# Chunk-selected attention into a gMLP block on one core: scores and masks in row halves, bounds of eight heads in eight tiles, x^T by DMA transpose, and a fixed order table

## The chip, the cores, the metric

One NeuronCore of a Trainium2 chip runs the whole kernel. The metric is device time in microseconds (us). A kernel is run several times, and each run is slow when it is over 1.5% above the fastest run of the same kernel, otherwise fast. A ratio is the mean time of one kernel's fast runs over that of the other's fast runs of the same rounds, so it is not quite the ratio of the medians quoted beside it. The kernel before has a profile (262.9 us) whose run isn't among the times listed.

Engines: PE is the matmul engine (PEld its weight loads), DVE the vector engine, ACT the activation engine, POOL the general engine, and SP issues most DMAs.

## The reference, cut to what matters

```python
# attention: B=4, H=8, S=768, D=64, chunks of 32 keys, the best 6 chunks of each query
k_min, k_max = k_chunks.min(3), k_chunks.max(3)
ub = sum(maximum(q * k_min, q * k_max), -1)          # bound of every (query, chunk)
ub = where(causal_by_chunk, ub, -1e9)
top_chunks = argsort(ub)[..., -6:]
scores = q @ k.T / 8, masked to chosen chunks and to causal positions
attn = softmax(scores) @ v
# gMLP on x = heads side by side, (4, 768, 512)
h = gelu(x @ w_in); u, v = halves of h
v_s = w_sg @ (layernorm(v) * g_ln) + b_sg
out = x + (u * v_s) @ w_out
```

Two heads of one batch make a *pair*; there are 16 pairs and 4 batches. Queries 0 to 191 have at most 6 chunks and need no selection. The other 576 do.

## The kernel before

Every piece of work is an `Op` with an engine, an estimated cost, and what it reads and writes. While the program is built, a scheduler plays these operations forward with the estimated costs and fixes each engine's order. Engines then run in that order and wait on semaphores, so a late operation holds up everything behind it on its engine. The rule is greedy: each engine takes what can start first. Priority decides only among operations that could start within 0.02 us of each other.

```python
# schedule(), cut: one engine's choice
for i in ready[e]:
    t = max(rt[i], free[e])                     # inputs there, engine free
    if o.alloc is not None and o.alloc.slot is None:
        s = slot_for(o.alloc, t)                # earliest free PSUM buffer of the allowed ones
        if s is None: continue
        t = max(t, s[0] + 0.15)
    cands.append((t, o.prio, i))
tmin = min(c[0] for c in cands)
best = min((c for c in cands if c[0] <= tmin + 0.02), key=lambda c: c[1])
```

PSUM has two large score buffers (PSC) and four small ones (PSG). Stages may use only some of the small ones, for instance (0, 1) for transposes and (2, 3) for the gMLP.

The scores carry the mask inside the contraction. `QA` has 64 rows of q and 24 rows of "this chunk is not chosen" (D); `KA` has 64 rows of k and 24 indicator rows. One matmul of 88 rows does a piece of a head. The second head of the pair uses 128 rows. The exp then runs over 1024, 1024 and 640 columns.

```python
# head(), cut
kt_, qt_, rows = (KA[w], QA[w], slice(0, 64 + NC)) if i == 0 else (KB[w], QB[w], slice(0, 128))
e.matmul(t.ap()[:, o:o + n], kt_[rows, 128*kb:128*kb+128], qt_[rows, q0:q0+n], start=True, stop=True)
...
# select(g), cut: bounds of 4 heads in 4 tiles of 64 rows x 32 columns, f32
for m in range(2):
    for j in range(4):
        w, lo = (2*g + j//2) % 4, 64 * (j % 2)
        e.matmul(t.ap()[32*j:32*j+32, 0:n], W[w][lo:lo+64, m, :], rhs, tile_position=(lo, 32*j), ...)
...
# xtrans(b, dk), cut: x^T by 6 PE transposes and a DVE copy
e.matmul(t.ap(BF16)[:, 128*j:128*j+128], XS[...], identB[:], is_transpose=True)
d.tensor_copy(xT[b % 2][:, dk, :], t.ap(BF16)[:, 0:S])
...
# weights(h), called after head(h): two of 14 weight loads wait for the first exp of head h
reads=[("tick", h)]
```

The softmax here doesn't subtract the row's maximum and nothing guards it: scores larger than these inputs give would overflow.

## Time and profile before

| | before |
|---|---|
| device time, median (range) | 267.67 us (266.84 to 268.25, 3 runs) |
| span of the profile | 262.9 us |
| busy PE / DVE / ACT / POOL | 225.0 / 197.7 / 153.4 / 76.9 us |
| start of the first and of the last exp | 23.8 and 227.9 us |

The first view is the page: busy time by engine, then the span in 40 slices of 6.6 us. A digit is the busy share in tenths. PEclk is the clock that PE was granted.

```profile
span 262.9 us, 5801 instructions
...
PE 225.0 (86%) x2242; PEld 140.2 (53%) x2258; DVE 197.7 (75%) x561; ACT 153.4 (58%) x232; POOL 76.9 (29%) x99
...
PE   8886488987996599998899899997998998689874
...
PEclk9999689999999569999999999999999999999999
DMA  7999999998999904856751443122101031100033
```

PE is at 9 in 18 of the 40 slices. No engine is full throughout, yet PE and DVE both carry most of the span, and the clock falls twice. The same as a table of stretches: stretch, its length, then busy us (and instructions) of PE, PEld, DVE, ACT, POOL, then granted clock, DMA share, GB/s.

```profile
core 0: us, PE busy (x) PEld busy (x) DVE busy (x) ACT busy (x) POOL busy (x), PEclk, DMA share, GB/s
...
20.00:40.00 20.00, 13.11 (x138) 7.96 (x137) 15.27 (x52) 11.82 (x20) 9.17 (x12) 0.83 1.06 208
...
80.00:100.00 20.00, 14.85 (x125) 9.90 (x123) 13.64 (x29) 12.34 (x19) 6.96 (x7) 0.74 0.67 123
...
140.00:160.00 20.00, 18.91 (x217) 13.53 (x211) 18.20 (x54) 14.29 (x22) 7.16 (x8) 1.00 0.38 92
```

PE loses time in 20-40 and 80-100 us, at a clock of 0.83 and 0.74. PE's busy time overstates its work, because matmuls overlap: six of 384 columns stream in 0.98 us, though each is listed with some 335 ns. DMA is near full for the first 14 slices, 92 us (208 GB/s in 20-40 us).

Three stages can be told apart by the exps. From the view of one source line (count, min/median/max ns, first and last start in us, shapes):

```profile
L682 ACT ACTIVATE E<-PSC x96: 698/1023/1074, 23.8 to 227.9; 128x1024 bf16<-128x1024 f32 x64, 128x640 bf16<-128x640 f32 x32
```

So the *start* takes 23.8 us, the *middle* 204.1 us, and the *end*, after the last exp starts, 35.0 us. The chain of waits through the start (start, length, what) is mostly DVE work in a row:

```profile
10.22 0.88 DVE KA L491
...
16.47 2.19 PE PSG L613 x32
...
19.20 1.47 DVE m_0 L629 x18
...
22.28 0.77 DVE QA L640
...
23.86 0.77 DVE QA L640
```

It runs on through four transposes of 0.77 us that write the mask rows into QA and QB. Score matmuls start at 23.11 us and the exp at 23.8 us.

### The profile page before, as it was taken

The numbers are of one execution on the slowest core, as the hardware profiler recorded it, in microseconds if no ns is written. First come the engines' busy times: TensorE is split into PE (matmuls) and PEld (weight loads), VectorE is DVE, ScalarE is ACT, GpSimd is POOL, SyncE is SP. The second block draws the span as 40 slices with busy tenths as digits, with TensorE's granted clock in tenths as the row PEclk, the third lists the DMA queues.
The fourth block names the chain that finished last, engine by engine and source line by source line (L and its number), as shares of the span: only waits on it lengthen the run. The fifth ranks groups of instructions, "written<-read, shape, count | busy, mean of one in ns | idle before, by whom it ended". The sixth has DMA issues, their size and how long they took to land.

```text
span 262.9 us, 5801 instructions
## 1 busy us (share of the span) xinstructions
PE 225.0 (86%) x2242; PEld 140.2 (53%) x2258; DVE 197.7 (75%) x561; ACT 153.4 (58%) x232; POOL 76.9 (29%) x99
## 2 busy tenths in 40 slices
PE   8886488987996599998899899997998998689874
PEld 3444256665743378655555577566445765434431
DVE  6949579787558668989677988886588876467883
ACT  1444848977649545655784974658757645846000
POOL 3353728653201424222212433134210211202000
PEclk9999689999999569999999999999999999999999
DMA  7999999998999904856751443122101031100033
GB/s 167 201 225 202 205 221 197 235 227 175 199 209 160 212 19 109 228 132 182 163 122 43 100 100 135 51 95 55 38 6 24 2 122 58 64 0 0 0 123 120
DMA packets 84652, 32.39 MB, mean 123 GB/s; under 512 B 77232, under 2 KB 80912, under 8 KB 84624
## 3 DMA queue, kind: packets, MB, share of 16 engines
q1 hardware_dynamic: 82608, 29.26, 48.1%
q0 software_dynamic: 2016, 2.75, 6.4%
q8 instruction: 18, 0.29, 0.5%
q14 instruction: 10, 0.08, 0.1%
HBM read 24.77 MB, written 6.29 MB: 118 GB/s over the span
## 4 chain that ended last, share of the span: by engine, by line
PE 50%; DVE 32%; ACT 9%; issue 6%; POOL 1%; POOLq 1%
PE PSG L794 9%; PE PSG L814 8%; PE PSC L677 8%; PE PSG L613 7%; DVE W L546 5%; ACT E L682 5%; DVE vhat L767 5%; PE PSG L751 4%; PE PSG L696 4%; DVE vsT L801 3%; PE PSG L777 3%; DVE uT L805 3%; DVE m_1 L629 2%; DVE XS L713 2%; PE PSC L463 2%
## 5 line engine op out<-in xcount | busy, mean ns | idle before, releaser
L682 ACT ACTIVATE E<-PSC 128x1024 bf16<-128x1024 f32 (+1 forms) x96 | 84.5, 920 | 44.7 <-PE PSC L677 44.1
L686 POOL TENSOR_SCALAR_AFFINE_SELECT E<-E 128x768 bf16<-128x768 bf16 x32 | 28.5, 892 | 59.9 <-ACT E L682 59.6
L794 PE MATMUL PSG<-wsgT,vhat 128*128 128x384 bf16 x192 | 36.6, 335 | 4.9 <-DVE vhat L767 3.0
L546 DVE TENSOR_REDUCE W<-PSG 128x12 f32<-128x384 f32 x64 | 33.1, 543 | 7.5 <-PE PSG L540 7.3
L677 PE MATMUL PSC<-QB,KB 128*128 128x128 bf16 (+1 forms) x224 | 26.0, 253 | 2.7 <-ACT E L682 2.7
L677 PE MATMUL PSC<-QA,KA 88*128 88x128 bf16 (+1 forms) x224 | 24.8, 249 | 3.4 <-ACT E L682 2.6
L794 PEld LDWEIGHTS PSG<-wsgT,vhat 128*128 128x128 bf16 x192 | 18.3, 100 | 17.6 <-DVE vhat L767 3.0
L801 DVE SCALAR_TENSOR_TENSOR vsT<-PSG,glnT,bsgbc 128x384 f32<-128x384 f32 x32 | 19.7, 614 | 7.6 <-PE PSG L794 7.5
L814 PE MATMUL PSG<-woutb,uT 128*128 128x512 bf16 x88 | 21.8, 380 | 3.9 <-DVE uT L805 3.3
L777 PE MATMUL PSG<-xT,winb 128*128 128x384 bf16 x128 | 23.8, 327 | 0.4 <-DVE xT L727 0.3
L696 PE MATMUL PSG<-vx,E 128*128 128x65 bf16 x480 | 20.4, 195 | 4.1 <-ACT E L682 2.7
L696 PEld LDWEIGHTS PSG<-vx,E 128*128 128x128 bf16 x480 | 18.0, 99 | 10.0 <-ACT E L682 5.6
L751 PE MATMUL PSG<-winb,xT 128*128 128x512 bf16 x90 | 21.6, 379 | 1.3 <-DVE xT L727 0.9
L575 PE MATMUL PSG<-identF,qn 128*128 128x128 f32 x96 | 16.1, 283 | 6.7 <-ACT KB L551 3.6
L755 ACT ACTIVATE vgb<-PSG 128x512 f32<-128x512 f32 x24 | 14.1, 598 | 13.1 <-PE PSG L751 13.1
L820 DVE TENSOR_TENSOR osb<-PSG,XS 128x512 f32<-128x512 f32 x24 | 16.6, 691 | 6.4 <-PE PSG L814 5.9
L677 PEld LDWEIGHTS PSC<-QA,KA 88*128 88x128 bf16 x224 | 16.3, 99 | 9.5 <-ACT E L682 4.6
L580 ACT ACTIVATE qT<-PSG 128x384 f32<-128x384 f32 x32 | 15.5, 496 | 9.5 <-PE PSG L575 9.4
L782 ACT ACTIVATE uT<-PSG 128x384 bf16<-128x384 f32 x32 | 15.6, 490 | 9.1 <-PE PSG L777 8.8
L598 POOL CAST vx<-vn 128x768 bf16<-128x768 f32 x16 | 13.2, 830 | 24.1 <-PE PSG L703 19.2
L677 PEld LDWEIGHTS PSC<-QB,KB 128*128 128x128 bf16 x224 | 15.9, 100 | 7.8 <-ACT E L682 4.9
L758 DVE BATCH_NORM_STATS2 stats<-vgb 128x6 f32<-128x512 f32 x24 | 16.0, 681 | 4.7 <-ACT vgb L755 4.7
(69 smaller groups left out, 343.7 us busy)
## 6 DMA issues: line engine op xcount, KB each, us to landing
kn<-in_k_dram SPq DMA_DIRECT2D x32, 192.0 KB, 3.6
qn<-in_q_dram SPq DMA_DIRECT2D x32, 192.0 KB, 3.6
vn<-in_v_dram SPq DMA_DIRECT2D x32, 192.0 KB, 3.5
out_dram<-osb SPq DMA_DIRECT2D x24, 256.0 KB, 2.0
vgb<-in_moe_w_sg_dram POOLq DMA_DIRECT2D x6, 192.0 KB, 5.9
QB<-QA SPq DMA_DIRECT2D x12, 96.0 KB, 2.2
KB<-KA SPq DMA_DIRECT2D x12, 96.0 KB, 3.0
winb<-in_moe_w_in_dram POOLq DMA_DIRECT2D x4, 256.0 KB, 5.9
```

What stands on the lines that cost most here:

```text
L546: P.op("dve", lambda d, t=t, m=m, op=op, hf=hf: d.tensor_reduce(W[w][:, m, 12 * hf:12 * hf + 12], t.ap()[:, 0:TG].rearrange("p (c x) -> p ...
L613: r = e.matmul(t.ap()[32 * j:32 * j + 32, 0:n], W[w][lo:lo + 64, m, :], rhs, start=(m == 0), stop=(m == 1), tile_position=(lo, 32 * j))
L677: r = e.matmul(t.ap()[:, o:o + n], kt_[rows, 128 * kb:128 * kb + 128], qt_[rows, q0:q0 + n], start=True, stop=True, skip_group_check=True)
L682: P.op("act", lambda e, t=t, c0=c0, c1=c1: e.activation(E[es][:, c0:c1], t.ap()[:, 0:c1 - c0], ACTF.Exp, scale=SCALE), act(c1 - c0), reads ...
L686: P.op("pool", lambda g: g.affine_select(ev, ev, pattern=[[0, NT], [1, 128]], compare_op=ALU.is_ge, fill=0.0, base=0, channel_multiplier=- ...
L696: r = e.matmul(t.ap()[:, 65 * qb:65 * qb + 65], E[es][:, a:a + 128], vx[w][:, kb, i, :], start=first, stop=False, skip_group_check=True)
L751: r = e.matmul(t.ap()[:, 0:F], xT[s][:, dk, 128 * qt:128 * qt + 128], winb[:, dk, F:DFF], start=(dk == 0), stop=(dk == NDK - 1))
L777: r = e.matmul(t.ap()[:, 0:TG], winb[:, dk, 128 * fb:128 * fb + 128], xT[s][:, dk, TG * tg:TG * tg + TG], start=(dk == 0), stop=(dk == NDK ...
L794: r = e.matmul(t.ap()[:, 0:TG], vhat[s][:, sb, 128 * fb:128 * fb + 128], wsgT[:, sb, TG * tg:TG * tg + TG], start=(sb == 0), stop=(sb == N ...
L801: P.op("dve", lambda d, t=t, fb=fb, tg=tg, vs=vs: d.scalar_tensor_tensor(vsT[vs][:], t.ap()[:, 0:TG], glnT[:, fb:fb + 1], bsgbc[:, TG * tg ...
L814: r = e.matmul(t.ap()[:, 0:DM], gT[s][:, fb, 128 * qt:128 * qt + 128], woutb[:, fb, :], start=(fb == 0), stop=(fb == NF - 1))
L820: P.op("dve", lambda d, t=t, qt=qt, os_=os_: d.tensor_tensor(osb[os_][:], t.ap()[:, 0:DM], XS[:, (b % 2) * NT + qt, :], op=ALU.add), dve(D ...
```

## The change

The intent, as its words give it (`window` is how many loads may be in flight; `filler` is how many dummy matmuls PE runs before an operation): both heads of a pair are done at once in the two halves of PE's rows, the mask is added by separate matmuls, bounds of eight heads use eight tiles, three of four x^T go to the DMA, and the order of all 1171 operations comes from a table found offline. Cut to its core:

```diff
+PLAN = dict(order=[0, 2, 47, 13, 6, ...],        # 1171 operations; cut
+            slots=[4, 5, 6, 7, ...],             # PSUM buffer of every tile, in that order; cut
+            window=4, filler={50: 7, 42: 3, 59: 11, 35: 7, 73: 7, 113: 4})
-    def schedule(self):                          # the greedy rule
+    def place(self, order, slots, window):       # takes the table as it is
 # scores of a pair, in six chunks of 2 x 512 columns (the last 2 x 128)
-    e.matmul(t.ap()[:, o:o+n], kt_[rows, ...], qt_[rows, ...], start=True, stop=True)
+    for i in range(2):
+        rows = slice(64*i, 64*i+64)
+        e.matmul(ap(t)[:, i, o:o+n], KT[r][rows, ...], QT[r][rows, q0:q0+n],
+                 start=True, stop=not masked, tile_position=(64*i, 0))
+    for i in range(2):
+        if masked:                               # queries from 192 on
+            e.matmul(ap(t)[:, i, o+m0-q0:o+n], IND[jj][rows, ...], D[ds][tb][rows, ...],
+                     start=False, stop=True, tile_position=(64*i, 0))
 # bounds: after two groups of four heads, groups of eight
+    ts = [PsumTile(ANY) for _ in banks]
+    ... tile_position=(64*i, 32*c)
 # x^T
+    if b > 0:
+        e.dma_start_transpose(xT[:, dk, :].rearrange("p (j x) -> p j x", x=128), flat(b, dk))
 # small PSUM buffers: every stage may take any of the four
-    t = ps_g.tile((2, 3))
+    t = PsumTile(ANY)                            # ANY = (4, 5, 6, 7)
 # weight loads, now declared before the first exp
+    for i in range(14):
+        weight(i)                                # reads=[("tick", 0)]
+    small_weights()                              # reads=[("tick", 0)]
```

Further: six sets of K, Q and V instead of four, one x^T and one normalized-V buffer instead of two, no copies KB<-KA and QB<-QA and their DMAs, and fewer memsets and copies at the start.

## The prediction

> **What bounds it now.** No single engine. The busy table gives PE 225 us (86%), DVE 198, ACT 153, POOL 77 of a 263 us span, but PE's figure contains pipeline latency: in the timeline six 384-column matmuls stream in 0.98 us (163 ns each) although one is listed as 335 ns. My estimate of PE work from stream spacings: gMLP 92 us, scores 36, probabilities times V 21, q/k transposes 20, bounds 15.5, x^T 5, w_sg 2; about 191 us. The other 70 us is dependency time:
> - Start: the first exp comes at about 23.8 us (timeline), behind a serial DVE chain that ends in four 0.77 us transposes into QA/QB (chain of waits).
> - First 80 us: the windows view shows DMA share about 1.0 at some 205 GB/s. About five pairs of q/k/v (1.18 MB each) and 5.4 MB of weights must arrive before the first gMLP: estimated 55 us. No order removes that.
> - Middle: granted clock 0.83 in 20-40 us and 0.74 in 80-100 us (windows); around 86-94 us PE waits on vhat.
> - Tail: last exp ends 228.6 us, then 34 us of the last gMLP alone.
>
> **What the change does.**
> - Bounds: 16 f32 matmuls with 288 columns take 0.97 us on four tiles; eight heads in eight tiles should take the same. Groups fall from eight to two of four heads and three of eight: 15.5 to 9.7 us of PE, minus 6.
> - Scores: mask rows move out of the contraction into separate matmuls, two heads running in row halves. Per pair 2688+2432 columns instead of 2x2688: at most 5% less if halves overlap. The Trainium skill, "TensorEngine Tiling (Array Packing)", Key Properties, says tiles run in parallel but changing mode drains the array. The trace agrees on both: the four bound tiles share 0.24 us slots, and the first weight load after a bound group starts about 0.14 us after the stream's end, after 0.47 us idle of the loader. With 96 score chunks and up to two switches each I estimate plus 15 to 30 us of PE, partly hidden. This is the main cost.
> - x^T: 12 of 16 PE transposes (0.34 us of PE) and DVE copies (0.55 us) go to DMA: PE minus 4, DVE minus 6.6. It happens when DMA share is below 0.65; costs a few us latency before each gMLP.
> - DVE also loses QA/QB transposes and setup copies: about 198 to 182.
> - ACT: same exp elements and instruction count (153 to about 150). Causal select on POOL: same elements.
> - Copies KB<-KA, QB<-QA and their small DMAs disappear.
> - Order: all four small PSUM buffers open to all stages, six K/Q/V sets, measured durations behind the table. I expect the largest gain here: middle stalls of about 40 us shrink by 10 to 15.
>
> **Sum (estimate).** Start -3, bounds/x^T/DVE -6 to -8 on the chain, order -12, mode switches +4: about -19 of the profile. Predicted time **247 us**, 80% range **231 to 263**. Faster by over 2%: 0.80; within 2%: 0.13; slower by over 2%: 0.07.
>
> **What would show it.** First exp before 22 us; score matmuls of two heads starting within a few ns, chunk streams about 0.4 us; an idle gap of 0.1 to 0.3 us around each score chunk; eight bound matmuls sharing a slot; DVE busy near 182, ACT near 150; fewer PE waits on ACT and vhat; tail still about 33 us; DMA still saturated to about 60 us.
>
> **What would make it wrong.** Row halves not overlapping (PE +34 us: no gain); larger drain; DMA transposes blocking loads in the SP queue or landing late; a fixed order mistimed so that in-order engines wait on each other; conversely a well packed order reaching 230 or less.

## The result, and the profile after

| | before | after |
|---|---|---|
| device time, median (range) | 267.25 us (263.39 to 268.25, 4 runs) | 241.84 us (238.98 to 245.76, 4 runs) |
| ratio of fast runs | | 0.902 (95%: 0.891 to 0.913) |
| span of the profile | 262.9 us | 236.6 us |
| start / middle / end by the exps | 23.8 / 204.1 / 35.0 us | 30.0 / 167.9 / 38.7 us |
| busy PE / DVE / ACT / POOL | 225.0 / 197.7 / 153.4 / 76.9 us | 216.4 / 182.3 / 149.0 / 72.0 us |

The medians after are of two fast and two slow runs, so the interval is wide. The profile after is a fast run. Its page:

```profile
span 236.6 us, 6378 instructions
...
PE 216.4 (91%) x2596; PEld 132.6 (56%) x2596; DVE 182.3 (77%) x531; ACT 149.0 (63%) x224; POOL 72.0 (30%) x99
...
PE   7739699999899399999999999999999999999974
...
PEclk9967999999999999999999999999999999999999
DMA  7899999999989999999740302043301411302143
```

```profile
core 0: us, PE busy (x) PEld busy (x) DVE busy (x) ACT busy (x) POOL busy (x), PEclk, DMA share, GB/s
...
20.00:40.00 20.00, 17.28 (x221) 11.27 (x223) 14.53 (x48) 11.07 (x20) 5.44 (x9) 0.99 1.08 208
...
80.00:100.00 20.00, 18.06 (x260) 12.21 (x258) 16.59 (x35) 17.63 (x26) 7.80 (x9) 1.00 0.98 200
...
140.00:160.00 20.00, 20.00 (x348) 12.19 (x348) 17.12 (x71) 14.83 (x20) 7.41 (x10) 1.00 0.22 52
```

```profile
L572 ACT ACTIVATE E<-PSC x96: 378/1023/1138, 30.0 to 197.9; 128x1024 bf16<-128x1024 f32 x80, 128x256 bf16<-128x256 f32 x16
```

PE is now at 9 in 32 of the 40 slices, and busy for the whole of 140-160 us. PEclk is at 9 from the fifth slice (24 us) on; in 80-100 us it is 1.00 in place of 0.74. DMA is near full for 19 slices, 112 us, in place of 92. The six buffer sets in place of four would let the loads run ahead so; no run isolates that.

By stages the 26.3 us of the span come from the middle alone: minus 36.2 us there, plus 6.2 us at the start, plus 3.7 us at the end. The chain of waits shows what happened at the start:

```profile
4.72 10.59 DMA qn<-in_q_dram
...
15.40 1.51 PE PSG L434 x6
...
22.85 2.19 PE PSG L495 x32
...
25.70 1.46 DVE m L513 x18
```

The second pair's q was issued at about 4.7 us and landed at 15.3, after 10.59 us. In the kernel before, that pair's k was transposed from 10.7 us and its q from 12.5 us; after, its q from 15.4 us and its k from 19.7 us. In between, POOL issued six of the weight loads (4.8 to 10.7 us), which share the DMA engines (DMA share 0.95 in 0-20 us). The chain also still has one mask transpose of 0.78 us (28.28 us) before the first exp, as before had.

That the weights go so early has its reason in the tick. The weight loads name it as something that they read, and should so wait for the exp that writes it. But they are declared before the exp that writes it, so there is no writer to wait for. The dependence turns round: the exp that writes the tick has to wait until all 16 readers are done. The built program says so; this is its ACT order (position, line, instruction, semaphores; cut):

```
29 L231 EventSemaphore [waits d_winb3,d_woutb2]
30 L231 EventSemaphore [waits d_winb2,d_winb0]
31 L231 EventSemaphore [waits d_woutb3,d_winb1]
32 L231 EventSemaphore [waits d_gln,d_woutb1]
33 L231 EventSemaphore [waits d_bsg,d_woutb0]
34 L572 Activation E<-PSC 128x2x512 [waits s_pe]
```

It is the eighth exp in ACT's order, not the first. In the trace it starts at 39.13 us, and the five waits before it take 0.04 us each: in this table the loads had landed by then. (The six w_sg loads aren't listed: the wait for PE covers them, as PE has transposed them by then.) So what delays the start is that nothing holds the weights back, not this wait.

The row halves overlap as hoped. A timeline of PE (start, length with latency, what; "x2" merges two):

```profile
100.75 1.14 PE L688 MATMUL PSG<-wsgT,vhat 128*128 128x384 bf16 x6
101.82 0.23 PE L556 MATMUL PSC<-QT,KT 64*128 64x128 bf16 x2
101.89 0.22 PE L563 MATMUL PSC<-D1Z,IND 64*128 64x128 bf16 x1
...
102.06 0.27 PE L556 MATMUL PSC<-QT,KT 64*128 64x256 bf16 x2
102.17 0.24 PE L563 MATMUL PSC<-D1Z,IND 64*128 64x192 bf16 x1
...
102.34 0.55 PE L434 MATMUL PSG<-identF,kn 128*128 128x128 f32 x3
```

Two heads' matmuls start together, each pair of 128 columns takes 0.06 us, and the w_sg group before it streams six times 0.163 us. That group ends its stream at 100.75 + 0.98 = 101.73 us; the scores begin at 101.82. The last mask matmul, 192 columns, ends its stream at about 102.25, and the next transpose begins at 102.34. So a change of array mode costs about 0.09 us either way. From 40 us on, the trace has 103 changes between the full array and the row halves that follow a bf16 matmul; their median gap is 95 to 98 ns, against 3 ns between matmuls of the full array. The Trainium skill, "TensorEngine Tiling (Array Packing)", Key Properties, says that changing the mode drains the array; this trace agrees and gives the size.

Bounds before (four heads) and after (eight heads), from the same view:

```profile
137.01 0.69 PE L613 MATMUL PSG<-qT,W 64*32 64x288 f32 x8
137.52 0.67 PE L613 MATMUL PSG<-rT,W 64*32 64x288 f32 x8
138.12 1.47 PE L777 MATMUL PSG<-xT,winb 128*128 128x384 bf16 x8
```

```profile
107.41 0.71 PE L495 MATMUL PSG<-qT,W 64*32 64x288 f32 x16
107.92 0.69 PE L495 MATMUL PSG<-rT,W 64*32 64x288 f32 x16
108.55 0.34 PE L556 MATMUL PSC<-QT,KT 64*128 64x384 bf16 x2
```

The interval to the next work is 1.11 us for 16 instructions before and 1.14 us for 32 after. Eight tiles run at the price of four.

### The profile page after: what moved, and what is told of

It is laid out like the page before. It is cut to its first block, busy times and chain, and to the rows that moved or that the text cites. A ratio compares the mean times of both kernels' runs of the same rounds, so it can differ in the third digit from the quotient of the medians.

```text
span 236.6 us, 6378 instructions
## 1 busy us (share of the span) xinstructions
PE 216.4 (91%) x2596; PEld 132.6 (56%) x2596; DVE 182.3 (77%) x531; ACT 149.0 (63%) x224; POOL 72.0 (30%) x99
## 4 chain that ended last, share of the span: by engine, by line
PE 71%; DMA 18%; DVE 4%; ACT 3%; SPq 2%; issue 1%
PE PSG L688 13%; PE PSC L556 9%; PE PSG L708 8%; DMA qn<-in_q_dram 8%; PE PSG L590 8%; PE PSG L434 7%; PE PSG L672 7%; PE PSG L645 7%; PE PSC L563 6%; DMA vn<-in_v_dram 5%; PE PSG L495 4%; DMA D1Z<-D1Y 2%; ACT E L572 2%; DMA kn<-in_k_dram 2%; DMA xT<-XS 2%; PE PSC L362 1%
## 5 line engine op out<-in xcount | busy, mean ns | idle before, releaser
L556 PE MATMUL PSC<-QT,KT 64*128 64x128 bf16 (+2 forms) x448 | 42.5, 246 | 4.8 <-ACT E L572 2.4
L578 POOL TENSOR_SCALAR_AFFINE_SELECT E<-E 128x512 bf16<-128x512 bf16 (+1 forms) x32 | 28.1, 884 | 31.1 <-ACT E L572 30.9
L556 PEld LDWEIGHTS PSC<-QT,KT 64*128 64x128 bf16 x448 | 20.3, 94 | 22.6 <-ACT E L572 9.3
L471 POOL CAST QT<-qT 128x768 bf16<-128x768 f32 x16 | 14.4, 898 | 47.0 <-ACT qT L465 35.7
L708 PE MATMUL PSG<-woutb,uT 128*128 128x512 bf16 x96 | 23.7, 380 | 1.3 <-DVE uT L699 1.3
L590 PE MATMUL PSG<-vx,E 128*128 128x65 bf16 x672 | 24.8, 194 | 0.0
L590 PEld LDWEIGHTS PSG<-vx,E 128*128 128x128 bf16 x672 | 22.2, 98 | 3.6 <-issue 1.4
L676 ACT ACTIVATE uT<-PSG 128x384 bf16<-128x384 f32 x32 | 15.5, 491 | 12.5 <-PE PSG L672 12.1
L434 PE MATMUL PSG<-identF,qn 128*128 128x128 f32 x96 | 15.1, 289 | 7.6 <-DMA qn<-in_q_dram 5.6
L450 ACT ACTIVATE KT<-PSG 128x384 bf16<-128x384 f32 x32 | 15.2, 498 | 10.0 <-DVE W L447 9.7
L699 DVE TENSOR_TENSOR uT<-vsT,uT 128x384 bf16<-128x384 f32 x32 | 20.9, 654 | 0.6
```

Of the source, the lines that this page charges most:

```text
L434: r = e.matmul(ap(t)[:, 128 * j:128 * j + 128], src[:, 3 * hf + j].rearrange("p i d -> p (i d)"), identF[:], is_transpose=True)
L556: x = e.matmul(ap(t)[:, i, o:o + n], KT[r][rows, 128 * kb:128 * kb + 128], QT[r][rows, q0:q0 + n], start=True, stop=not masked, tile_posit ...
L578: P.op("pool", lambda g, ev=ev, nd=nd: g.affine_select(ev, ev, pattern=[[0, 2], [0, nd // 128], [1, 128]], compare_op=ALU.is_ge, fill=0.0, ...
L590: x = e.matmul(ap(t)[:, 65 * qb:65 * qb + 65], E[es][:, i, a:a + 128], vx[r][:, kb, i, :], start=first, stop=(kb == qb), skip_group_check= ...
L699: P.op("dve", lambda d, fb=fb, tg=tg, vs=vs: d.tensor_tensor(uT[s][:, fb, TG * tg:TG * tg + TG], vsT[vs][:], uT[s][:, fb, TG * tg:TG * tg ...
L708: r = e.matmul(ap(t)[:, 0:DM], uT[s][:, fb, 128 * qt:128 * qt + 128], woutb[:, fb, :], start=(fb == 0), stop=(fb == NF - 1))
```

## The experiments

Twelve kernels ran on three chips. Where a number is compared across chips, the ratio to before is used. The kernel after stands at 0.902 by its own runs. e4, which turned out to be its equal in time, stands at 0.909.

### e1: the new operations in the old order

The edit puts the operations of the kernel after through the greedy rule of the kernel before, and stores the resulting order, buffers and filler as its table.

```diff
-    order=[0, 2, 47, 13, ...], slots=[4, 5, 6, 7, ...],        # the table of the change
-    filler={50: 7, 42: 3, 59: 11, 35: 7, 73: 7, 113: 4})
+    order=[...], slots=[...],                                  # the greedy rule's
+    filler={31: 9, 40: 3, 50: 14, 59: 6, 71: 4})
```

> The kernel after with its operations unchanged, but order, buffer slots and filler taken from the greedy rule of the kernel before instead of the searched table. Theory A (most of the gain is the searched order): 254 to 264 us, so less than half of the 25 us remains. Rival B (the new operations make the gain, any sensible order will do): 247 us or less. The 96 exps should again be spread over 190 us or more from first to last under A, and 175 us or less under B (before 204, after 168).

Measured: 284.12 us median, ratio 1.070 (1.064 to 1.076). That is 42 us more than e4 on the same chip, and slower than before.

```profile
L573 ACT ACTIVATE E<-PSC x96: 377/1024/1142, 35.3 to 243.6; 128x1024 bf16<-128x1024 f32 x80, 128x256 bf16<-128x256 f32 x16
```

The middle is 208.3 us, no shorter than before's 204.1. Rival B falls. Theory A's direction holds, but not its size: the new operations in the old order do not keep a part of the gain; they lose 18 us. The whole gain, and more, came with the table. Changes of array mode are not what makes e1 slow: its PE order has 107 of them, the table's 146. One thing isn't separated: e1 keeps the turned tick, so the greedy rule had to place that exp behind all 16 weight loads. The greedy rule without the tick was not run.

### e2: scores without row halves and mask matmuls (wrong numbers on purpose)

```diff
-    e.matmul(ap(t)[:, i, o:o+n], KT[r][rows, ...], QT[r][rows, ...], tile_position=(64*i, 0), stop=not masked)
-    e.matmul(... IND ..., ... D ...)             # the mask
+    e.matmul(ap(t)[:, i, o:o+n], KT[r][:, ...], QT[r][:, ...], start=True, stop=True)   # all 128 rows
```

> Wrong numbers on purpose: each score matmul uses all 128 rows (5376 columns a pair, no mask matmuls, no row halves), same table. It takes away 2 changes of array mode for each of 96 chunks, 0.09 us each by the trace (17 us of PE together), and adds about 1.7 us of columns. Theory: PE is what limits from 80 us on, so the time falls by 8 to 16 us, to 226 to 234. Rival: the drains hide behind other waits, time within 2 us of the kernel after.

Measured: 233.89 us, ratio 0.878 (0.874 to 0.883); 7.9 us less than e4 on the same chip. The result was wrong. The table lets score chunks follow each other at places, so that PE changes mode not 192 but 146 times (147 runs of one mode in its order). e2 keeps 16 of these, for the bounds, and takes away 130. At 0.09 us that is 12 us; 7.9 us plus the 1.7 us of added columns is about 10 us. The rest may hide behind waits, or in the clock: in 80-120 us the profile of e2 was granted 0.91, that of e4 1.00. So row halves cost this kernel 8 us against a score of the same size on the full array. A correct version of that would again need masks and both heads' rows copied together, as in the kernel before; it was not built.

### e3: one half after the other in program order

```diff
-    for (o, n, kb, q0) in todo:
-        for i in range(2): ...score...
-        for i in range(2): ...mask...
+    for i in range(2):
+        for (o, n, kb, q0) in todo: ...score... ...mask...
```

> Same matmuls as the kernel after and right numbers, but in each chunk all of head 0's come before all of head 1's, so that neighbours in the queue share a row half and cannot overlap. If the overlap of the halves is what makes the scores affordable: score streams double from 34 to 68 us and the time rises by 20 to 34 us, to 262 to 276, no better than before. Rival (halves overlap little, or PE has slack): rise under 8 us.

Measured: 244.36 us, ratio 0.918 (0.913 to 0.924), 2.6 us above e4 on the same chip. This was a miss, but not because overlap is worth little. The edit did not take it away:

```profile
29.82 0.23 PE L557 MATMUL PSC<-QT,KT 64*128 64x128 bf16 x2 [1.80 <-DVE D0X L521]
29.88 0.22 PE L561 MATMUL PSC<-D0X,IND 64*128 64x128 bf16 x2
29.94 0.22 PE L557 MATMUL PSC<-QT,KT 64*128 64x128 bf16 x1
```

In this first chunk the program order, in the built program too, is score and mask of head 0, then score and mask of head 1. The trace has the scores of both heads at 29.82 us and both masks at 29.88. The second head's matmul started before the first head's mask that stands ahead of it. The Trainium skill, "TensorE: Matmul & The Clock Gate", Part 3, says that matmuls keep strict program order in start and end. This trace differs in the start, and the measurement decides: matmuls of another row half went ahead. (Ends of matmuls are modelled in these profiles and say nothing here.) e12 repeats the test properly.

### e4: without the tick

```diff
-            after = [("tick", 0)]
+            after = []
```

> The reads of the tick are dropped from the 16 weight loads. In the kernel after they were declared before the exp that writes the tick, so they do not hold the weights back: instead one exp of the first pair waits for all 16 loads. Same table. Theory: that wait is short (the searched order put the weights early because of it), time lower by 0 to 3 us; first exp still at about 30 us since the second pair's q and k still share the DMA with the weights. Rival (the wait holds up the start): lower by 4 to 7 us.

Measured: 241.80 us, ratio 0.909 (0.904 to 0.914). The wait of the exp costs nothing in this table, as its 0.04 us waits in the trace after suggested. The rival falls. First exp 31.3 us, as expected.

### e5: without the tick, and the weights later in the table

```diff
             after = []                           # as in e4
     order=...                                    # the 16 weight loads one after every second q/k/v load
                                                  # from the 9th on; w_sg transposes before the first hidden matmul
```

> Tick reads dropped as in e4, and the table changed for the weights alone: the 16 weight loads and the w_sg transposes are taken out of the first 30 us; w_sg and w_in come between the loads from the 9th q/k/v load on, one for every two, b_sg, g_ln and w_out after them, the w_sg transposes right before the first hidden matmul. Theory (the slow start is the weights sharing the DMA with the second pair's q and k): first exp at 20 to 25 us in place of 30; the total falls by 2 to 6 us, to 236 to 240, less than the start because the first gMLP still waits for the same bytes. Rival (the first 70 us are bound by total DMA bytes, the start is hidden): earlier first exp, total within 1.5 us of 241.8, or later if the moved transposes stall PE.

Measured: 239.64 us, ratio 0.8965 (0.893 to 0.900). This is the fastest correct kernel. It ran on another chip than e4, so its margin of about 1% is likely rather than shown.

```profile
L573 ACT ACTIVATE E<-PSC x96: 378/1024/1131, 20.9 to 196.9; 128x1024 bf16<-128x1024 f32 x80, 128x256 bf16<-128x256 f32 x16
```

The start fell from 30.0 to 20.9 us, which shows that the weights made it slow. But 9 us at the start gave some 2 us in all, since the middle grew from 167.9 to 176.0. Its chain of waits tells why:

```profile
12.80 6.60 DMA kn<-in_k_dram
...
22.93 10.93 DMA qn<-in_q_dram
33.88 4.20 DMA kn<-in_k_dram
```

Up to 54 us the chain goes on so: loads of q, k or v are its long links. The same bytes must come before the same work; attending to the first pair earlier only leaves PE waiting later (in 40-60 us it is busy for 14.54 us, after for 19.72). Both theories had a share: the cause of the late start was the weights, and the rival was right that the total is bound by bytes there.

### e6 and e11: x^T of all batches back on PE and DVE

```diff
-            if b > 0:
-                P.op("sp", lambda e: e.dma_start_transpose(...))
+            if False:
     order=..., slots=...     # 12 x (6 PE transposes, a DVE copy) put in; e11 where a buffer stays free longer
```

> x^T of batches 1 to 3 back on PE and DVE (6 transposes of 0.056 us and a 0.55 us copy for each of 12 tiles), put into the searched table two PE steps after the place of the DMA. Theory: PE is the limit from 80 us on, so the time rises by 3 to 6 us (PE 4.1, DVE 6.6), to 245 to 248. Rival (the DMA transposes delay the gMLP by their 3.3 us landing; the wait at 165 us in the trace is one): no rise, or a fall of up to 3 us.

> As e6 (x^T of batches 1 to 3 on PE and DVE again) but placed with more care: the transposes where a buffer stays free longest, the copy after two more DVE operations. If e6's 12 us were mostly mistimed waits of my insertion: 246 to 250 us. If the work itself, 10.7 us on two nearly full engines, costs it: 252 us or more.

Measured: e6 253.91 us, ratio 0.949 (0.944 to 0.953). e11 247.13 us over all runs, two of which are slow; its ratio of fast runs is 0.919 (0.911 to 0.926). So e6 came out above both of its expectations. e11 met its first by all runs, and its two fast runs (244.11 and 245.14 us) are just below it. The same operations at slightly different places of the table differ by about 8 us. In e6 the weight loads before the w_sg matmuls waited for my copies (total us, times, longest):

```profile
PEld PSG L690 <- DVE xT L624: 4.9, 6, 0.8
```

e6 therefore says little about x^T. Against after's 0.902 and e4's 0.909, e11 suggests that the DMA transposes are worth 1 to 2%, and its interval touches both others. It does confirm how sensitive the table is to its exact content. Issues from the page after (count, KB each, median us to landing):

```profile
kn<-in_k_dram SPq DMA_DIRECT2D x32, 192.0 KB, 3.8
...
xT<-XS SPq DMA_TRANSPOSE x12, 3.3
```

The Trainium skill, "Advanced Engine Details and Errata", X-Bar Transpose (TRN2), says that transpose DMAs are as fast as regular ones. Each transpose moves 192 KB (128 x 768 x 2 bytes), as much as a load. Where both run, in 94-112 us, this trace agrees: a median of 4.4 us for 3 transposes, 3.7 us for 4 loads of k and 4.5 us for 9 of v. In 160-236 us, where DMA is quiet, it doesn't bear it out: 2.8 us for 6 transposes, 2.0 us for 16 stores of 256 KB. But those go to HBM, and no run has a plain copy of the same path.

### e7 and e8: single parts of the change in the kernel before

```diff
 # e7: any stage may take any small PSUM buffer
-            t = ps_g.tile((2, 3))            # and the other restrictions
+            t = ps_g.tile()
 # e8: x^T of batches 1 to 3 by DMA, XS laid out for it
+            if b > 0:
+                P.op("sp", lambda e: e.dma_start_transpose(xT[b % 2][:, dk, :]..., XS[:, b % 2, dk]...)); return
```

> The kernel before with one edit: every stage may take any of the four small PSUM buffers, as in the kernel after; the greedy rule orders as before. If the open buffers alone give part of the gain: 250 to 262 us. Rival (under a greedy rule open buffers let the gMLP crowd out transposes and probabilities times V, as e1 suggests): 268 to 285 us.

> The kernel before with x^T of batches 1 to 3 by DMA transpose alone (greedy rule reorders around it). PE minus 4, DVE minus 6.6 us of work, but neither is saturated in the kernel before: theory 262 to 267 us, within 2%. Rival (the prediction's share of 'bounds, x^T, DVE: minus 6 to 8'): 259 to 262 us.

Measured: e7 261.72 us, ratio 0.980 (0.975 to 0.985); e8 264.10 us, ratio 0.988 (0.982 to 0.993). Open buffers alone give 2%, so the rival of e7 falls. x^T by DMA alone gives 1.2%, within 2% as expected. These are gains of 5 and 3 us under the greedy rule, which also reordered everything around the edit. As e6 and e11 differ by 8 us through placing alone, 3 us can't be put down to the DMA itself.

### e9 and e10: both sets of operations in the order of one search

The search was mine. It starts from the priorities, changes them at random, lets a list scheduler place all operations under a rough model with the costs of each kernel's own file, and keeps what is better: 13 minutes on four processors, about 30,000 trials each, once for each kernel. e9 uses the old operations with the open buffers of e7, e10 the new ones with the tick as it is.

```diff
 # e9, in the kernel before
-        P.schedule()
+        P.place(ORDER, SLOTS, FILLER, idle)      # table from the search
 # e10, in the kernel after
-    order=..., slots=..., filler=...             # the table of the change
+    order=..., slots=..., filler=...             # table from the search
```

> The operations of the kernel before, unchanged (open buffers as in e7, every cross-engine order inside a buffer kept), but its order, buffer slots and filler come from a table too: my own search, 13 minutes of random changes of priorities under a rough model. Theory A (the searched order is the gain, the new operations add nothing that a good order does not already give): 238 to 250 us, at least half of the 25 us. Rival B (order and new operations are needed together): 255 us or more.

> The operations of the kernel after with the order from the same search with the same effort, in place of the table that came with the change. It says how good my search is against that table, and with e1 and e9 completes the square of operations and orders. Under A: 244 to 258 us, no better than e9. Under B: below e9 by 8 us or more.

Measured: e9 246.76 us, ratio 0.924 (0.918 to 0.929). e10 262.79 us, ratio 0.987 (0.982 to 0.992). Both ran on the same chip.

```profile
L772 ACT ACTIVATE E<-PSC x96: 698/1018/1085, 22.9 to 210.0; 128x1024 bf16<-128x1024 f32 x64, 128x640 bf16<-128x640 f32 x32
```

```profile
L574 ACT ACTIVATE E<-PSC x96: 378/1023/1098, 43.0 to 225.5; 128x1024 bf16<-128x1024 f32 x80, 128x256 bf16<-128x256 f32 x16
```

The old operations with open buffers in a searched order keep 20 of the 25 us; the open buffers alone gave 5 (e7). Their middle is 187.1 us in place of 204.1. Theory A holds for e9, and rival B falls. e10 is worse than A expected, and its lines say where: the first exp comes at 43.0 us. Its chain at the start:

```profile
6.36 18.29 DMA qn<-in_q_dram
24.69 1.54 PE PSG L436 x6
```

A q load took 18.29 us beside the weights, which my model has cheaper than they are (2.0 us for a load of w_in, whose median landing took 7.3 us after). The new operations put nothing in the way of early weights; with the turned tick, they even make one exp wait for all of them, and my search had to obey that. No search ran without the tick, so its part in e10 stays open. Its middle, 182.5 us, is 4.6 us shorter than e9's. So in the middle the new operations are a little better at equal effort, and at the start much worse.

The square of operations and orders, as ratios to before:

| | greedy rule | my search | the table of the change |
|---|---|---|---|
| old operations, open buffers | 0.980 (e7) | 0.924 (e9) | not possible |
| new operations | 1.070 (e1) | 0.987 (e10) | 0.902 (after) |

### e12: both heads in one row half (wrong numbers on purpose)

```diff
-                            rows = slice(64 * i, 64 * i + 64)
-                            ... tile_position=(64 * i, 0)
+                            rows = slice(0, 64)
+                            ... tile_position=(0, 0)
```

> Wrong numbers on purpose: both heads of a pair use rows 0 to 63 and the tile position of the first half, so that no two score matmuls can overlap; same instruction count, same table. The overlap was not taken away in e3 (its trace shows the halves still running side by side). Score streams 34 to 68 us: time up by 20 to 34 us, 262 to 276 us, if the overlap is worth its columns; up by under 8 us if PE has slack for it.

Measured: 277.71 us, ratio 1.042 (1.035 to 1.049): about 37 us above after, if after's ratio is applied to the 267.19 us of before in these rounds. That is a little above the expected range, which ended at 276. Two score matmuls of 256 columns now follow each other:

```profile
111.48 0.38 PE L556 MATMUL PSC<-QT,KT 64*128 64x256 bf16 x2
111.70 0.33 PE L563 MATMUL PSC<-D1X,IND 64*128 64x192 bf16 x2
```

The next pair of matmuls starts 0.22 us after this one, where the timeline of after has 0.11 us from the pair of 256 columns to the mask behind it (102.06 to 102.17). Both stretches have a granted clock of 1.00. So the halves overlap fully: together they stream in half the time. Without overlap of the halves the change would have been slower than before, as the prediction feared.

## Why the prediction was right or wrong

The total was right: 241.84 us measured, 247 predicted with 231 to 263. The direction and the main term, "I expect the largest gain here" of the order, were right. Several terms of the sum were mis-sized, and they offset each other, so that the total came so close is in part luck.

- **"Start -3": wrong in sign.** The first exp came at 30.0 us in place of 23.8. I had counted the four mask transposes that disappear. But only one of them came before the first exp (22.28 us, exp at 23.8 us), and the kernel after still has one there (28.28 us), so nothing was to be gained from them. And I had not counted that the weights might take the DMA from the second pair's loads. e5 shows that cause by undoing it: first exp at 20.9 us. It also shows that the start hid behind the DMA: 9 us there were worth some 2 us in total.
- **"order -12": far too small.** The middle fell by 36.2 us. e1 shows that without the table nothing of this remains, and e9 that the old operations get 17 us of it from open buffers and a search of 13 minutes. I had taken the waits of the trace for what order could remove. My reading, which no run isolates, is that the greedy rule also let clock, DMA lead and PE backlog go to waste, which no single wait shows.
- **"bounds/x^T/DVE -6 to -8 on the chain": removed as work, not shown as time.** DVE busy is 182.3 us (predicted near 182), ACT 149.0 (near 150), bounds run eight for the price of four. But the same operations under the old rule cost 18 us (e1). x^T by DMA came with 3 us in the kernel before (e8), less than placing alone can do. What the eight-head bounds are worth alone was not tested.
- **"mode switches +4": too small.** The drain is 0.09 us, just under the stated 0.1 to 0.3 us. With PE as the limit, little of it hides: e2 gives 8 us net.
- **Overlap of halves:** right, shown in the trace and by e12.
- **"DMA still saturated to about 60 us":** wrong; it is near full to 112 us. The end after the last exp starts went from 35.0 to 38.7 us; the expected 33 us for the tail was counted from the exp's end and came out somewhat low.

What stays open: how far the old operations would go with a search as good as that of the change, whose table beats mine by some 22 us on the new operations (0.902 against 0.987); and how much of the loss of e1 and e10 is due to the turned tick, and of e10 to the model's cheap weights. The experiments show that order makes the gain and that the change's table and operations fit each other. They do not show which of the two, at its best, would win.

## What to carry to other kernels

When a kernel is built as a list of operations with a fixed order per engine, try a searched order on the old operations first: here that was 20 of 25 us, open buffers included. Judge new operations together with an order made for them, because under the old rule less work on DVE, ACT and POOL (180.9, 149.4 and 73.0 us busy in e1, against 197.7, 153.4 and 76.9 us before) became a loss of 18 us. And check that a dependence is declared after its writer: declared before, it silently turns round.

## What the Trainium skill lacked or had wrong

- "TensorE: Matmul & The Clock Gate", Part 3: it says that matmuls keep strict program order. In e3, matmuls of the other row half started ahead of earlier ones of the first half (both heads' scores at 29.82 us, masks at 29.88 us, against the program order score, mask, score, mask), and putting the halves apart cost only 2.6 us.
- "TensorEngine Tiling (Array Packing)", Key Properties: the drain at a change of mode has no size there. Here it was about 0.09 us at each change (101.73 to 101.82 us and 102.25 to 102.34 us after), with a median of 95 to 98 ns over 103 changes of that trace. Taking away 130 of the 146 changes, with the mask matmuls, gained 7.9 us net (e2).
